# Attention loop: second halves of side work an iteration later, routing in mid-iteration, part of a weight conversion moved into the next stage

## The chip, the cores and the metric

One core of one Trainium2 chip runs the whole program. The time is device microseconds of one execution; the profile comes from one further execution with the hardware profiler on. TensorE (PE) multiplies matrices, VectorE (DVE), ScalarE (ACT) and GpSimd (POOL) work on rows, SyncE (SP) and POOL issue most of the transfers. Each engine works through its own queue in order.

## What is computed

Three layers follow one another. The first is a recurrent attention over 4 sequences of 768 tokens with 8 heads of 48:

```python
for t in range(S):
    cur = u * k_t (outer) v_t
    y_t = r_t @ (state + cur)
    state = w_t[:, None] * state + k_t (outer) v_t
```

The second is a mixture of 8 experts where each of the 3072 tokens (rows of 384) goes to the expert with the largest gate logit: `out = gate_w * (relu(x @ w1[e]) @ w2[e])`, with w1 of 384 x 1024. The third is a mixture of the same sizes in which each token goes to its two best experts by noisy logits. Inputs and outputs are float32.

## The kernel before, in words

Attention works on blocks of 128 tokens: 24 blocks (`NT`), 6 per sequence (`NC`). One loop, `for i in range(-4, NT)` in `attention`, runs as a pipeline by hand: iteration i transposes inputs of block i+3 and i+4, makes decays (two scans on VectorE) of block i+3, decayed keys and receptances ("products") of block i+2, scores of block i+1 on TensorE, their copies ("am", ScalarE) and masks (POOL), and the outputs and the state of block i: `ps` (state matmuls, line 452), `py` (line 457 from the carried state S, line 459 from the scores). `sums` writes the finished block into X, and the block's transposes (`turn`, line 497) and gate matmuls (`logits`, line 221) come one and two iterations later. The first block of a sequence has no carried state.

The order of the instructions in the text sets the order of every engine's queue there. At the end of each iteration stand the steps of `todo` and of `extra`:

- `todo` is the routing of a finished sequence b. `route1a` has four steps, in iterations 7 to 10 for the first sequence and six later for each next one: logits plus bias and the row maximum; the one-hot of the first maximum, the subtraction and the exponential (ScalarE); the ranks (small TensorE matmuls), the running count `seen` and the sum of the exponentials; the slot index. `route1c` scatters one block's rows to the table R1 (POOL).
- `extra` holds preparation of the first visit of layer two. `first_a`, `first_b`, `first_c` (from iteration `FI`) pick the largest expert of the first sequence from a count matmul (line 262). The steps in iterations `GW` are gathers of its weights w1 and w2 by POOL, that in `N0` the count of its tokens. The steps in iterations `EC` convert these weights: two squares (line 794, ScalarE), a total (two tiny TensorE matmuls, line 207), scales (VectorE) and then splits into two float16 halves, three for w1 and four for w2. A split is a ScalarE operation (line 812, the high part) and a VectorE operation (line 815, the low part). The steps in iterations `EX` fetch the visit's 448 rows: a gather by POOL (line 864), the scales (lines 195 to 199, VectorE) and four parts, each a ScalarE operation (line 226), a VectorE operation (line 227) and a transposing transfer on SP's queue (line 903).

A step with two halves returns its second half as a function. `once` calls the step and then, at once, what it returned.

After attention come seven visits of layer two (448 rows of one expert each; 8 blocks of first matmuls, line 834, then second matmuls, line 849), and then layer three. In a visit, work beside the matmuls is put into numbered slots, one after each block, and second halves run one slot later than their first. What `EC` has left of the conversion goes into the slots given to `spread`. The last sequence's routing stands in the first visit's slots 2, 3, 6 and 6.

Of the kernel before, what the change touches and what calls it, by code (L numbers as in the profile page):

```python
# [58 lines left out]
OE = 1  # L59
WI = -4  # L60
GI = (1, 2, 5, 8)
FI = 9
GW = (11, 12, 13, 16)
N0 = 15
EC = (15, 16, 17, 18, 18, 19, 20, 21, 22, 23, 23)
S1 = 3
EX = (19, 20, 20, 21, 21, 22)
FE = 1
# [15 lines left out]
def kernel(  # L84
# [163 lines left out]
    def ranks(x, m16, n, pr):  # L248

        nc.tensor.matmul(pr, tri, m16, start=True, stop=False)  # L250
        for c in range(n - 1):
            nc.tensor.matmul(pr[:, c + 1:, :], ones, bc(m16[:, c:c + 1, :], [P, n - 1 - c, E]),
                             start=False, stop=False)
        nc.tensor.matmul(pr, ones, bc(seen[x][:, None, :], [P, n, E]), start=False, stop=True)
        with nc.allow_low_precision(reason="counts up to 48 are exact"):
            sums = small.tile([P, E], F16, name="sums")
            nc.vector.tensor_reduce(sums, m16.rearrange("p c e -> p e c"), axis=AX, op=OP.add)
            nc.vector.tensor_tensor(seen[x], seen[x], sums, op=OP.add)
# [47 lines left out]
    def attention(extra):  # L306

        with ExitStack() as st:
# [173 lines left out]
            def norm(t):  # L482
                b, c = divmod(t, NC)
                sq = keep.tile([P, D], F16, name="sq")
                nc.scalar.activation(sq, row(t)[:, 0:META].bitcast(F32), AF.Square,
                                     accum_out=row(t)[:, META:ROW].bitcast(F32)[:, SS:SS + 1])
                if c == NC - 1:
                    meta = X[b % 2][:, :, META:ROW].bitcast(F32)
                    nc.gpsimd.tensor_copy(meta[:, :, 0], tok_all[:, b * NC:(b + 1) * NC])
                    nc.gpsimd.tensor_copy(meta[:, :, 2:2 + E], noise_sb[:, b * NC:(b + 1) * NC, :])  # L490
# [16 lines left out]
            def route1a(b, x):  # L507

                sh = [P, NC, E]
                if x == 0:  # L510
                    R = RB[b] = {n: small.tile(s, d, name=f"r1{n}") for n, s, d in (
                        ("lg", sh, F32), ("ex", sh, F32), ("oh16", sh, F16), ("sm", [P, NC], F32),
                        ("ri", sh, F32), ("rf", [P, NC], F32), ("idx", [P, NC], I32))}
                    nc.vector.tensor_tensor(R["lg"], pl[b % 2], bias_all[:, b * NC:(b + 1) * NC, :], op=OP.add)
                    R["mx"], R["oh"], R["fm"] = first_max(R["lg"], NC, "r1")
                    R["fm"][0]()
                    return
                R = RB[b]
                if x == 1:
                    for f in R["fm"][1:]:  # L520
                        f()
                    nc.vector.tensor_tensor(R["lg"], R["lg"], bc(R["mx"][:, :, None], sh), op=OP.subtract)
                    nc.gpsimd.tensor_copy(R["oh16"], R["oh"])
                    nc.scalar.activation(R["ex"], R["lg"], AF.Exp)
                elif x == 2:
                    ranks(0, R["oh16"], NC, pr[b % 2])
                    nc.vector.tensor_reduce(R["sm"], R["ex"], axis=AX, op=OP.add)
                    nc.vector.tensor_scalar(R["sm"], R["sm"], 1e-9, None, op0=OP.add)
                    nc.vector.reciprocal(X[b % 2][:, :, META:ROW].bitcast(F32)[:, :, 1], R["sm"])
                else:  # L530
                    nc.vector.tensor_tensor(R["ri"], pr[b % 2], bc(erow[:, None, :], sh), op=OP.add)
                    nc.vector.tensor_tensor(R["ri"], R["ri"], R["oh"], op=OP.mult)
                    nc.vector.tensor_reduce(R["rf"], R["ri"], axis=AX, op=OP.add)
                    nc.vector.tensor_copy(R["idx"], R["rf"])
# [23 lines left out]
            def at(f, t):  # L558
                if 0 <= t < NT:
                    f(t)  # L560

            for i in range(-4, NT):
                for n, g in enumerate(data):
                    if i >= GI[n]:
                        next(g, None)
                if i >= 0:
                    at(scores, i + 1)
                at(norm, i - 1)
                at(products, i + 2)
                at(decays_a, i + 3)  # L570
                if i >= 0:
                    at(scores_out, i + 1)
                    at(masks, i + 1)
                at(logits, i - LG)
                at(decays_inv, i + 3)
                at(decays_b, i + 3)
                if i == -2:
                    scores(0)
                    scores_out(0)
                    masks(0)  # L580
                    if OE:
                        keys_back(0)
                o = {-1: 0, 0: -1}.get(i, i) if OE else i
                at(outputs, o)
                at(diag, i + 2)
                at(state, o)
                at(turn, i - 1)
                if i >= KB and (i >= 0 or not OE):
                    at(keys_back, i + 1)
                at(state_out, o)  # L590
                at(diag_v, i + 2)
                at(sums, o)
                for n, t in (("kr", i + 3), ("w", i + 4)):
                    at(lambda t: transposes(t, n), t)
                if 0 <= i < KB:
                    keys_back(i + 1)
                if i == WI:
                    warm(WARM[1])
                at(loads_q, i + 3)
                if i >= -2 and i + NL + 2 <= NT:  # L600
                    load(i + NL + 2)
                if i >= 0:
                    nc.sync.dma_start(out[i * P:(i + 1) * P, :], zt)
                for at_i, f, b, x in todo:
                    if at_i == i:
                        f(b, x)
                for f in extra.get(i, []):
                    f()

            last = {"rows": [lambda: norm(NT - 1)], "turn": lambda pt: turn(NT - 1, pt),  # L610
                    "logits": [lambda t=t: logits(t) for t in range(NT - LG, NT)],
                    "route": [], "scatter": []}
# [559 lines left out]
    def layers():  # L1172
# [80 lines left out]
        steps0 = []  # L1253
# [3 lines left out]
            if callable(f):  # L1257
                f()

        def some(n):  # L1260
            for _ in range(n):
                once(steps0.pop(0))

        xsteps = []

        def begin(j, sidx):
# [2 lines left out]
        extra = {}  # L1269
# [3 lines left out]
                     (EC[0], lambda: steps0.extend(conv0()))):  # L1273
            add(extra, i, f)
        for i in EC:
            add(extra, i, lambda: some(1))
        for i in GW:
            add(extra, i, lambda: wsteps.pop(0)())
        for i in EX:
            add(extra, i, lambda: once(xsteps.pop(0)))  # L1280

        with tc.manual_schedule():
            last = attention(extra)
        with ExitStack() as st:
# [91 lines left out]
            with tc.manual_schedule():  # L1376
# [12 lines left out]
                for j in range(VISITS):  # L1389
                    hooks = {}  # L1390
                    q = max(0, j - EV + 1)
                    if j == 0:
# [11 lines left out]
                        add(hooks, S1 + 2, lambda: begin(1, early["sidx1"]))  # L1404
                        for s in XS1:
                            add(hooks, s, lambda: xsteps.pop(0)())
                        spread(hooks, steps0, (0, 1, 2, 3, 4, 5, 6))
                    else:
                        if j == 1:
                            for x, s in enumerate(T_PLAN):  # L1410
# [181 lines left out]
```

## Time and profile before

| | us |
|---|---|
| median of 3 runs | 882.61 (881.57 to 887.2) |
| the profiled execution's own time | 883.38 |
| its span, first to last instruction | 881.6 |
| TensorE busy | 841.1 (95%) |
| VectorE, ScalarE, POOL busy | 464.3, 435.0, 360.5 |
| attention's last iteration ends, first visit's first matmul | 211.06 |

The times of the rows count from the span's start. The span is 1.8 us shorter than the execution's time. The page's clock line gives TensorE's granted clock per fortieth of the span (22 us), 9 being full speed.

### The profile page before, as it was taken

The page shows a single profiled execution, that of the slowest core. Times are in us where ns is not written, and L with a number is a line of the kernel's source. Part 1 is how long each engine was busy: PE and PEld are TensorE (multiplying, and loading weights), DVE is VectorE, ACT ScalarE, POOL GpSimd, SP SyncE. Part 2 cuts the span into 40 slices and gives each one's busy share as a digit, 9 for nine tenths or more (in the row PEclk, how much of TensorE's full clock was granted, in tenths as well). Part 3 has the DMA queues.
Part 4 walks back from the last instruction along what each step waited for, and adds up shares of the span by engine and source line. Part 5 has one row for each costly group of instructions (what it writes and reads, how often), then busy time and mean ns, then how long its engine had stood idle before and what let it go on. Part 6 is the DMA issues. An engine that isn't in the chain of part 4 may idle for free.

```text
span 881.6 us, 16060 instructions
## 1 busy us (share of the span) xinstructions
PE 841.1 (95%) x6161; PEld 633.1 (72%) x6161; DVE 464.3 (53%) x1244; ACT 435.0 (49%) x819; POOL 360.5 (41%) x404
## 2 busy tenths in 40 slices
PE   7999999989999989899999999999999999999993
PEld 6989999888576566565666678667686766768672
DVE  7979779873674466458666624333332423333220
ACT  2545346554354475567776426445444634534220
POOL 7957697942333161540424642232122223212222
PEclk9999799966999989999999999999999999999997
DMA  9986487423454231743574384864756546535231
GB/s 178 196 154 148 108 223 165 157 64 89 123 184 112 57 103 42 244 127 100 194 223 94 80 249 95 229 179 101 197 102 198 90 86 176 102 54 102 56 38 20
DMA packets 195077, 115.42 MB, mean 131 GB/s; under 512 B 173499, under 2 KB 183863, under 8 KB 193585
## 3 DMA queue, kind: packets, MB, share of 16 engines
q1 hardware_dynamic: 169088, 63.82, 29.6%
q0 software_dynamic: 18224, 50.12, 22.8%
q10 hardware_dynamic: 7680, 0.38, 0.6%
q8 instruction: 50, 0.82, 0.4%
q14 instruction: 35, 0.28, 0.1%
HBM read 73.37 MB, written 30.01 MB: 117 GB/s over the span
## 4 chain that ended last, share of the span: by engine, by line
PE 86%; DVE 4%; issue 3%; ACT 2%; POOL 1%; DMA 1%; ACTq 1%; POOLq 0%; DVEq 0%
PE ph L834 33%; PE po L841 20%; PE po L849 10%; PE py L459 4%; PE pm L221 4%; PE pA L422 3%; PE py L457 2%; PE po L858 2%; PE pTk L377 1%; PE pTr L377 1%; PE pTw L377 1%; PE pA L439 1%; PE po L1112 1%; PE pA L497 1%; PE ps L452 1%
## 5 line engine op out<-in xcount | busy, mean ns | idle before, releaser
L834 PE MATMUL ph<-xT,w1h 128*128 128x320 f16 (+2 forms) x1104 | 290.9, 350 | 3.4 <-DMA xT<-xs 1.5
L959 DVE SCALAR_TENSOR_TENSOR hl<-ph,hh 128x320 f16<-128x320 f32 (+2 forms) x184 | 110.0, 599 | 238.2 <-ACT hh L958 222.0
L1150 POOL DMA_INDIRECT out_dram<-y,oidx x56 | 87.6, 1563 | 268.0 <-ACT y L1149 265.6
L834 PE MATMUL ph<-xT,w1l 128*128 128x320 f16 (+2 forms) x552 | 192.0, 348 | 1.0 <-issue 1.0
L834 PEld LDWEIGHTS <-w1h 128*128 128x128 f16 x1104 | 155.1, 146 | 45.8 <-issue 9.9
L958 ACT ACTIVATE hh<-ph 128x320 f16<-128x320 f32 (+2 forms) x184 | 95.4, 521 | 124.8 <-PE ph L834 102.2
L841 PE MATMUL po<-w2h,hh 128*128 128x384 f16 x384 | 125.2, 326 | 0.5 <-issue 0.5
L841 PE MATMUL po<-w2l,hh 128*128 128x384 f16 x384 | 125.2, 326 | 0.0
L841 PE MATMUL po<-w2h,hl 128*128 128x384 f16 x384 | 125.2, 326 | 0.0
L841 PEld LDWEIGHTS <-hh 128*128 128x128 f16 x768 | 74.2, 98 | 48.4 <-issue 1.0
L834 PEld LDWEIGHTS <-w1l 128*128 128x128 f16 x552 | 79.7, 144 | 24.6 <-issue 3.9
L1149 ACT ACTIVATE y<-po,gf 128x384 f32<-128x384 f32 (+1 forms) x56 | 31.6, 577 | 113.7 <-PE po L841 83.4
L1084 POOL DMA_INDIRECT R<-X,idx x56 | 56.3, 1006 | 22.3 <-issue 13.3
L815 DVE SCALAR_TENSOR_TENSOR w1l<-stage,ps_w,w1h 128x1024 f16<-128x1024 f32 x36 | 47.7, 1340 | 25.8 <-ACT w1h L812 25.8
L849 PE MATMUL po<-hh,w2h 128*128 128x448 f16 x168 | 59.9, 356 | 1.1 <-issue 1.1
L849 PE MATMUL po<-hl,w2h 128*128 128x448 f16 x168 | 59.8, 356 | 0.7 <-issue 0.7
L849 PE MATMUL po<-hh,w2l 128*128 128x448 f16 x168 | 59.7, 355 | 0.7 <-issue 0.7
L459 PE MATMUL py<-vt,am 128*128 128x48 f32 x384 | 59.3, 286 | 0.0
L432 POOL TENSOR_SCALAR_AFFINE_SELECT am<-am 128x512 f32<-128x512 f32 x48 | 46.6, 992 | 30.8 <-ACT am L427 30.7
L849 PEld LDWEIGHTS <-w2h 128*128 128x128 f16 x336 | 33.1, 99 | 34.6 <-issue 5.3
L459 PEld LDWEIGHTS py<-vt,am 128*128 128x128 f32 x384 | 55.8, 212 | 0.2
L841 PEld LDWEIGHTS <-hl 128*128 128x128 f16 x384 | 37.6, 98 | 24.9
(323 smaller groups left out, 1410.8 us busy)
## 6 DMA issues: line engine op xcount, KB each, us to landing
stage<-in_moe_w_dram SPq DMA_DIRECT2D x16, 1536.0 KB
ldw<-in_w_dram SPq DMA_DIRECT2D x24, 192.0 KB
ldk<-in_k_dram SPq DMA_DIRECT2D x24, 192.0 KB
ldr<-in_r_dram SPq DMA_DIRECT2D x24, 192.0 KB
vt<-in_v_dram SPq DMA_DIRECT2D x24, 192.0 KB
out_dram<-zt SPq DMA_DIRECT2D x24, 192.0 KB
R<-X,idx POOLq DMA_INDIRECT x56
xT<-xg SPq DMA_TRANSPOSE x56
```

What stands on the lines that cost most here:

```text
L221: nc.tensor.matmul(pl, xT[:, i, :], g[:, i, :], start=i == 0, stop=i == NI - 1)
L432: nc.gpsimd.affine_select(m, m, pattern=[[0, HP], [1, P]], compare_op=OP.is_gt, fill=0.0, base=0, channel_multiplier=-1)
L459: nc.tensor.matmul(PY[t][:, hp, x], AM[t][x][:, hp, :], VT[t][:, 2 * hp + x], start=c == 0, stop=c == 0 or x == 1)
L815: nc.vector.scalar_tensor_tensor(l, v, s, h, op0=OP.mult, op1=OP.subtract)
L834: nc.tensor.matmul(ph, a[:, i, :].rearrange("p (q m) -> p m q", m=NM)[:, m, :], xT[:, b, cols], start=n == 0, stop=n == 3 * NI - 1)
L841: nc.tensor.matmul(py, a[m][:, cols], b[:, m, :], start=n == 0, stop=n == 3 * NM - 1)
L849: nc.tensor.matmul(py, b[:, m, d * P:(d + 1) * P], a[m][:, cols], start=n == 0, stop=n == 3 * NM - 1)
L958: nc.scalar.activation(hh[m][:, 0:T], ph, AF.Relu)
L959: nc.vector.scalar_tensor_tensor(hl[m][:, 0:T], ph, 0.0, hh[m][:, 0:T], op0=OP.max, op1=OP.subtract)
L1084: st = nc.gpsimd.indirect_dma_start(out=R2[:, :], out_offset=bass.IndirectOffsetOnAxis(ap=R.idx[0:VP, x, h:h + 1], axis=0), in_=R.row[0:VP ...
L1149: nc.scalar.activation(y[0:n], py[0:n], AF.Copy, scale=gf[0:n, h:h + 1])
L1150: st = nc.gpsimd.indirect_dma_start(out=out[:, :], out_offset=bass.IndirectOffsetOnAxis(ap=oidx[0:n, h:h + 1], axis=0), in_=y[0:n], in_off ...
```

## The change

Second halves of the steps in `extra` are no longer run at once: the loop collects them in `second` and runs them in the middle of the next iteration, behind the scans and ahead of the outputs. The steps of `route1a` move from the iteration's end to the same place, its exponential moves from the second step to the third, and the sum and reciprocal of the exponentials from the third to the fourth. The scatters (`route1c`) stay at the end. The choice of the largest expert, its weight gathers and its count come one iteration later, and the conversion of its weights as well, with nine steps in attention instead of eleven: the total, the scales and all four splits of w2 are in the first visit, where before only the splits were, and the slots are 0, 1, 1, 2, 3, 4 instead of 0, 1, 2, 3.

```diff
-FI = 9
-GW = (11, 12, 13, 16)
-N0 = 15
-EC = (15, 16, 17, 18, 18, 19, 20, 21, 22, 23, 23)
+FI = 10
+GW = (12, 13, 14, 17)
+N0 = 16
+EC = (16, 17, 18, 19, 20, 21, 22, 23, 23)
...
                     nc.gpsimd.tensor_copy(R["oh16"], R["oh"])
+                elif x == 2:
                     nc.scalar.activation(R["ex"], R["lg"], AF.Exp)
-                elif x == 2:
                     ranks(0, R["oh16"], NC, pr[b % 2])
+                else:
                     nc.vector.tensor_reduce(R["sm"], R["ex"], axis=AX, op=OP.add)
                     nc.vector.tensor_scalar(R["sm"], R["sm"], 1e-9, None, op0=OP.add)
                     nc.vector.reciprocal(X[b % 2][:, :, META:ROW].bitcast(F32)[:, :, 1], R["sm"])
-                else:
                     nc.vector.tensor_tensor(R["ri"], pr[b % 2], bc(erow[:, None, :], sh), op=OP.add)
...
+            second = []
+
+            def flush():
+                for f in second:
+                    f()
+                second.clear()
...
                 at(decays_b, i + 3)
+                flush()
+                for at_i, f, b, x in todo:
+                    if at_i == i and f is route1a:
+                        f(b, x)
...
                 for at_i, f, b, x in todo:
-                    if at_i == i:
+                    if at_i == i and f is route1c:
                         f(b, x)
                 for f in extra.get(i, []):
-                    f()
-
+                    f = f()
+                    if callable(f):
+                        second.append(f)
+
+            flush()
...
-        def some(n):
-            for _ in range(n):
-                once(steps0.pop(0))
...
         for i in EC:
-            add(extra, i, lambda: some(1))
+            add(extra, i, lambda: steps0.pop(0)())
...
         for i in EX:
-            add(extra, i, lambda: once(xsteps.pop(0)))
+            add(extra, i, lambda: xsteps.pop(0)())
...
-                        spread(hooks, steps0, (0, 1, 2, 3, 4, 5, 6))
+                        spread(hooks, steps0, (0, 1, 1, 2, 3, 4, 5))
```

## Rows read from the trace of the kernel before

**Rows 1.** The page: busy time of each engine, and the granted clock in 40 slices.

```profile
PE 841.1 (95%) x6161; PEld 633.1 (72%) x6161; DVE 464.3 (53%) x1244; ACT 435.0 (49%) x819; POOL 360.5 (41%) x404
...
PEclk9999799966999989999999999999999999999997
```

**Rows 2.** Iterations: length; busy us of PE, PEld, DVE, ACT, POOL; PEclk; DMA share; GB/s.

```profile
127.89:135.15 7.26, 7.26 (x83) 6.89 (x82) 6.33 (x15) 3.69 (x10) 6.54 (x8) 1.00 0.94 240
...
94.33:105.88 11.55, 11.55 (x79) 11.01 (x78) 9.28 (x25) 3.28 (x9) 6.14 (x6) 0.56 0.44 103
...
143.28:150.02 6.74, 6.74 (x78) 6.40 (x78) 6.53 (x13) 3.20 (x8) 4.44 (x5) 1.00 0.57 141
156.84:164.87 8.03, 8.03 (x75) 7.66 (x74) 5.78 (x11) 4.71 (x11) 7.49 (x9) 0.79 0.71 274
164.87:174.09 9.22, 7.33 (x83) 6.89 (x82) 8.46 (x12) 3.81 (x11) 8.38 (x12) 1.00 0.13 46
174.09:184.15 10.06, 10.06 (x79) 9.53 (x78) 8.77 (x12) 4.34 (x9) 8.12 (x8) 0.66 0.25 83
184.15:195.79 11.64, 9.18 (x78) 8.62 (x77) 7.61 (x22) 7.82 (x16) 2.85 (x5) 0.75 0.11 32
195.79:204.50 8.71, 8.14 (x51) 7.65 (x50) 2.43 (x8) 3.04 (x8) 2.09 (x3) 0.50 0.34 64
204.50:211.06 6.56, 6.03 (x30) 5.95 (x31) 1.33 (x3) 2.38 (x7) 3.52 (x6) 0.50 0.54 181
211.06:214.00 2.94, 2.94 (x9) 1.39 (x9) 0.66 (x5) 0.47 (x2) 1.99 (x3) 0.53 0.18 70
```

**Rows 3.** What TensorE waited for, 80 to 260: total us, times, longest.

```profile
PE pA L497 <- ACT am L427: 2.5, 1, 2.5
PE pm L221 <- DVE r1lg L514: 1.9, 1, 1.9
...
PE pm L262 <- DVE seen L258: 1.3, 2, 0.8
```

**Rows 4.** VectorE in order of time: start, duration, instruction, idle before it.

```profile
164.91 2.85 DVE L815 SCALAR_TENSOR_TENSOR w1l<-stage,ps_w,w1h 128x1024 f16<-128x1024 f32 x1 [2.19 <-ACT w1h L812]
...
186.74 1.28 DVE L815 SCALAR_TENSOR_TENSOR w1l<-stage,ps_w,w1h 128x1024 f16<-128x1024 f32 x1 [1.35 <-ACT w1h L812]
```

**Rows 5.** ScalarE in order of time: a state copy, a split and a row part.

```profile
139.83 0.71 ACT L476 COPY S<-z 48x192 f32<-48x192 f32 x2
...
185.57 1.13 ACT L812 ACTIVATE w1h<-stage,ps_w 128x1024 f16<-128x1024 f32 x1
188.34 0.61 ACT L226 ACTIVATE xs<-xg,ps_g 112x384 f16<-112x384 f32 x1 [1.63 <-DVE ps_g L198]
```

**Rows 6.** VectorE in iterations 14 and 15: the first-maximum step, the state.

```profile
131.78 0.55 DVE L238 TENSOR_TENSOR c_r<-r1lg,mx_r 128x48 f32<-128x48 f32 x1
...
133.80 0.20 DVE L522 TENSOR_TENSOR r1lg<-r1lg,mx_r 128x48 f32<-128x48 f32 x1
...
138.61 0.36 DVE L470 TENSOR_TENSOR z<-ps,g 128x192 f32<-128x192 f32 x1
```

**Rows 7.** TensorE: first use of a state; first matmul of the second visit.

```profile
143.77 0.46 PE L457 MATMUL py<-S,RT 128*128 128x96 f32 x2
...
243.18 0.54 PE L834 MATMUL ph<-xT,w1h 128*128 128x448 f16 x2 [1.46 <-DMA xT<-xs]
```

**Rows 8.** POOL issues the row gathers of the first and second visit.

```profile
176.21 1.85 POOL L864 DMA_INDIRECT xg<-R,ev_sidx  x1
...
226.41 1.00 POOL L864 DMA_INDIRECT xg<-R,ev_sidx  x1 [3.78 <-DVE ev_n L1226]
```

**Rows 9.** A stretch of 2 us behind the first visit's gather, as rows 2.

```profile
180.00:182.00 2.00, 2.00 (x12) 1.67 (x12) 1.97 (x4) 0.56 (x1) 0.38 (x2) 0.50 0.73 299
```

**Rows 10.** VectorE in the first visit: scales and last row half for the second.

```profile
231.76 0.17 DVE L195 TENSOR_SCALAR pe_g<-xg 128x4 int32<-128x4 int32 x1 [1.58 <-DMA xg<-R,ev_sidx]
...
240.09 0.62 DVE L227 SCALAR_TENSOR_TENSOR xs<-xg,ps_g,xs 112x384 f16<-112x384 f32 x1
```

## The prediction

> **What bounds the kernel now.** I read the page's busy line and its clock line first [rows 1]. TensorE is busy for 95% of the span, so a change pays only where TensorE stands still or runs at its lower clock, and the clock line is low most often in the first quarter, which holds the attention loop. There I cut the trace at the first state matmul of each iteration and asked for busy time and granted clock of each piece [rows 2]. An undisturbed iteration takes 7.26 us (iteration 14) at clock 1.00, and 6.74 (iteration 16) where the four transposes of the keys are left out, so four transposes are 0.52. Against that the reader is to see three things: iteration 10 with 11.55 us at clock 0.56; iterations 12 and 18, the first of a sequence, which are alike and stand with one row, 8.03 at 0.79 with TensorE busy throughout; and iterations 19 to 23, which take 46.2 us together, with the clock at 0.50 over the last two. Then I listed what TensorE waited for [rows 3]: no wait over 2.5 us, but low clock follows them. Last I followed the queues of VectorE and ScalarE in iterations 18 to 21 [rows 4, 5].
>
> **Why they are late there.** Each step that splits w1 has a ScalarE half and a VectorE half that follows at once. VectorE stands 2.19 us for ScalarE, then takes 2.85 us, and all that is behind it is late [rows 4]; there are three such waits, of which the first and the last are shown. In iteration 19 the routing's subtract-and-max is behind that, and TensorE's next gate matmul waits 1.9 us for it [rows 3]. At the end of iteration 20 it is a ping-pong: VectorE waits 1.35 us for the split, only then makes the scales of the first visit's rows, ScalarE waits 1.63 us for these [rows 5], and the copies of the scores ("am") behind that hold TensorE's transposes for 2.5 us [rows 3]. After that the clock is half until the first visit.
>
> **The change, part by part**, against the profiled execution (883.38 us; the median of the runs is 0.8 lower).
>
> *First expert an iteration later.* The count matmul stood right behind the ranks, at the ends of iterations 9 and 15, and waited for VectorE's "seen": 1.3 us in two waits, 0.8 and 0.5 [rows 3]. Routing now comes half an iteration earlier and the count a full one later, so both waits go: 1.3 us. Behind the first the clock fell: iteration 10 has the work of iteration 16, so 11.55 - 6.74 = 4.8 us go if the fall was the wait's. The four weight gathers move an iteration later on POOL's queue. POOL is nearly full in iterations 18 and 19 (7.49 of 8.03, 8.38 of 9.22 [rows 2]), so it drags a backlog, but by then the same transfers have been issued in both kernels: nothing.
>
> *VectorE's halves an iteration later.* VectorE's three waits go, and the halves run in iterations 21 to 23, which have fewer products and scans. Iteration 19 falls from 9.22 to 7.26 (2.0). Iteration 20 has one group of transposes less: 10.06 to 6.74 (3.3). Iteration 21 has three groups less and the ranks (about 0.3): 7.26 - 1.56 + 0.3, about 6.0 instead of 11.64. On the old time axis iteration 20 then begins at 172.1, 21 at 178.9, 22 at 184.9.
>
> *What is late next.* VectorE now comes to the row scales much earlier, right behind the sums of iteration 20. In iteration 14 the routing starts, behind the sums, 3.9 us after the iteration's start; with 2.2 us of routing put ahead of them [rows 6] that is 172.1 + 6.1 = 178.2. But the rows are not there: POOL issues their gather at 176.21 [rows 8], and data still come at 299 GB/s in the stretch to 182 [rows 9], a landing 5.8 us after the issue; for the second visit it is 226.41 to 231.76, 5.4 us [rows 8, 10]. The issue took 1.85 there against 1.00 in the visit, so POOL may come 0.9 earlier; the rows land between 180.6 and 182, and VectorE stands 2.4 to 3.8 us. Behind it are some 5 us of its usual work and the split's half before the state of iteration 21 is out, near 186.7 with ScalarE's copy, where TensorE's output matmuls want it at 185.4: about 1 us. ScalarE waits for the scales too, and the copies of the scores behind it hold the transposes of iteration 21 by another 0.7 to 1.2. A third wait of about 1 us comes at iteration 23, where the state copy is behind two row halves (0.62 each [rows 10]), a split's half (1.28 [rows 4]) and routing.
>
> *The end of attention.* The last ScalarE half, VectorE half, row half, transpose and landing form a chain; from the end of the last row half to the first matmul it is 240.71 to 243.18 in the second visit, 2.5 us [rows 7, 10]. Without a fall of the clock the state copy of iteration 23 is out at 192.9, and two ScalarE halves (1.13 and 0.61), two VectorE halves (1.28 and 0.62) and these 2.5, partly overlapping, put the first matmul of the first visit at 198.4 instead of 211.06: 12.7 us less. With a fall at the end of iteration 21 the last two iterations take their present 15.3 us [rows 2], some 4 us of scores and gate matmuls stand ahead of them from 184 on, and it comes at 203.3: 7.8 less. I take a fall within iteration 22, at 202.1: 9.0, nearer to the second because the new waits stand where [rows 2] shows falls. The first visit begins at half clock now (2.94 us at 0.53 [rows 2]); after a wait for rows it will do so for a little longer, up to twice that: 0.8 taken off. On SP's queue the four row transposes pass a few zero writes and nothing else waits there: nothing.
>
> *Routing mid-iteration.* It puts 2.2 us (131.78 to 134.0) ahead of the state update. In the next iteration that update ends at 138.97 [rows 6], ScalarE's copy takes 0.71 [rows 5], and the state is used at 143.77 [rows 7]: 4.1 us of cover, of which 1.9 are left. Cost nothing; with the cover gone it is rival three. The exponential moves to the next step, so ScalarE no longer waits for it; in the first visit it stands in one slot with its sum, at most half a us of VectorE.
>
> *w2 in the first visit.* Its sum (two tiny matmuls), three small VectorE operations and the first split come a slot later, and the others with it. TensorE waits for nothing in that visit until 241.7 [rows 7], and the second half of the matmuls begins three slots behind the last split. Between 0 and 0.5; I take 0.
>
> **Sum:** 1.3 + 4.8 + 9.0 - 0.8 = 14.3; of 883.38 that leaves 869.1, on the median's basis 868.3. **Forecast 868.5.**
>
> **The rivals.** *One: the clock falls whatever the waits.* For it: iterations 12 and 18 fall with no idle at all, and the last iterations have few transposes to keep the array dense. Against it: iteration 15 has the same ranks with a shorter wait, and iteration 16 behind it stays at 1.00 [rows 2]. Then 1.3 us remain, and what iterations 19 and 20 give before a fall at the start of iteration 21 (first matmul at 206.4, 4.7 less): 6.0, so 876.6. The Trainium skill ("TensorE: Matmul & The Clock Gate", Part 1, the HAM clock gate) holds that the clock is gated down after TensorE has been idle for a spell, which a gap of 0.8 us hardly is; by that rule the fall in iteration 10 was not the wait's and would come back, as in this rival. The trace does not settle it: it shows a fall behind 0.8 us and falls behind none. Chance 0.20.
>
> *Two: the gathered rows become the bound.* If they land after 182, VectorE's stand is over 3.8 us, the scores' copies and the state of iteration 21 hold TensorE for 2 us or more, and the clock falls inside iteration 21. The first matmul comes near 206: 5 less instead of 9.0. With 1.3 + 4.8 that makes 11.1: 871.5. For it speaks POOL's backlog, against it the shorter issue. Chance 0.14.
>
> *Three, slower: routing ahead of the state.* If POOL stretches scans and routing beyond the cover, TensorE waits before its output matmuls in each iteration with the first-maximum step (8, 14, 20), and a fall like that of iteration 10 follows: 0.8 + 4.8 each, 17 us. The end stays at half clock as now, and only the 6.1 of the first part is saved: 893.5. It decides from 1.9 us of stretch, nearly the routing's own length again. Chance 0.06.
>
> That the halves are not deferred at all I give nothing: the three splits and four row parts return their second half, and only these.
>
> **How the numbers follow.** Forecast 0.60, rivals 0.20, 0.14, 0.06. The forecast's own range is 863.8 (no fall before iteration 23) to 872. Adding rival two and most of rival one: 862 to 878.5. Within 1% of 882.6 (about what a measurement of this kernel tells from no change) begins at 873.8: faster is 0.95 of the forecast, most of rival two and little of rival one, 0.67; same 0.27; slower 0.06.
>
> **What would show it.** Right: no wait for "seen"; iteration 10 at 6.7 to 7.3 us and clock 1.00; no VectorE wait for the split w1; VectorE's scale operation waiting for the gather; the first matmul of the first visit 12 to 19 us earlier than now. Wrong: iteration 10 at half clock again; TensorE idle before output matmuls in iterations 8, 14 or 20; iterations 21 to 23 again over 25 us together; or the first visit longer than its 30.5 us up to the wait for the second visit's rows.

## The result, and the profile after

The changed kernel takes 876.88 us (median of 11 runs, 870.34 to 879.4), the kernel before 883.17 beside it (11 runs, 880.48 to 887.2): ratio 0.9894 [0.9865, 0.9922], faster by 1.1%. The profiled execution took 870.34, the fastest of the 11; its span is 868.5 us at a mean granted clock of 0.970, against 883.38, 881.6 and 0.954 before. So what the profile shows is the changed kernel at its best: 13.0 us less, where the medians give 6.3 and the ratio 9.4 (0.0106 x 883.17). Here and below a ratio is taken over the fast runs alone, those within 1.5% of the kernel's fastest, while a median holds every run; on the third chip of the experiments this leaves 11 of 29 runs of the kernel before out of the ratios.

The page after, to be read beside [rows 1]: TensorE's busy time is 12.8 us less, and the clock line, which before falls to 7, 6 and 6 in slices 5, 9 and 10, stays at 8 or above in the first quarter (8 in slices 6, 9 and 10).

```profile
PE 828.3 (95%) x6161; PEld 621.0 (72%) x6161; DVE 472.1 (54%) x1244; ACT 436.1 (50%) x819; POOL 362.3 (42%) x404
...
PEclk9999989988999989999999999999999999999997
```

The span times the granted clock is 841.0 before and 842.4 after. At full clock the two profiled executions would be equally long; their difference is time at half clock (881.6 x 0.046 = 40.6 and 868.5 x 0.030 = 26.1).

Iterations of the changed kernel in the columns of [rows 2]: 10, 13, 18 to 23, and the start of the first visit.

```profile
92.40:99.66 7.26, 6.96 (x80) 6.61 (x80) 6.92 (x19) 3.13 (x9) 5.38 (x6) 1.00 0.64 138
...
113.58:124.33 10.75, 10.57 (x81) 9.97 (x82) 9.36 (x15) 6.30 (x16) 10.12 (x10) 0.68 0.65 160
...
153.36:159.79 6.43, 6.43 (x76) 6.16 (x75) 6.29 (x11) 2.81 (x9) 5.59 (x6) 1.00 0.42 156
159.79:168.67 8.88, 7.74 (x83) 7.04 (x82) 8.21 (x17) 5.16 (x12) 8.30 (x11) 1.00 0.56 202
168.67:179.19 10.52, 10.44 (x85) 9.77 (x84) 9.17 (x14) 4.18 (x10) 10.20 (x14) 0.68 0.30 99
179.19:185.88 6.69, 6.50 (x73) 5.87 (x70) 6.03 (x13) 4.21 (x11) 3.75 (x4) 1.00 0.11 26
185.88:192.52 6.64, 4.62 (x51) 4.25 (x50) 4.85 (x13) 4.87 (x12) 2.45 (x3) 0.90 0.33 85
192.52:199.11 6.59, 6.02 (x27) 5.76 (x28) 2.76 (x4) 2.66 (x6) 4.09 (x5) 0.50 0.62 210
199.11:202.05 2.94, 2.94 (x10) 1.51 (x10) 0.06 (x2) 2.94 (x5) 1.99 (x3) 0.59 0.18 70
```

Iteration 10 runs at full clock, iterations 21 and 22 take 13.3 us instead of 20.4, and the first visit starts at 199.11 instead of 211.06. Half clock is still there, in iterations 13, 20 and 23.

What TensorE waited for, 80 to 260, in the columns of [rows 3]:

```profile
PE py L457 <- ACT S L476: 1.6, 3, 1.3
...
PE pm L221 <- DVE pe_w L195: 0.8, 1, 0.8
PE pm L221 <- DVE r1ri L531: 0.8, 1, 0.8
PE ps L452 <- DVE z L470: 0.8, 1, 0.8
...
PE pm L221 <- DVE cnt_half L264: 0.6, 1, 0.6
PE pm L221 <- DVE cnt_first L264: 0.3, 1, 0.3
```

The waits of [rows 3] for am (2.5), r1lg (1.9) and seen (1.3) are gone; shorter ones stand in their place, two kinds for the state (S, z) and four of gate matmuls (line 221). `pe_w`, `r1ri` and the counts are what VectorE makes from other columns of the PSUM tile `pm` that the gate matmul writes, so in this program it waits for reads of results that it does not touch.

VectorE in order of time, as [rows 4, 10] (the low part of a split is line 829 here, the scales of the gathered rows line 195), and POOL's gather, as [rows 8]:

```profile
104.51 1.97 DVE L239 SCALAR_TENSOR_TENSOR c_ev<-c_ev,eio 128x8 f32<-128x8 f32 x1
...
169.21 3.46 DVE L386 TENSOR_TENSOR_SCAN g<-w,d1r 128x516 f32<-128x516 f32 x1
...
179.44 0.54 DVE L195 TENSOR_SCALAR pe_g<-xg 128x4 int32<-128x4 int32 x1 [1.40 <-DMA xg<-R,ev_sidx]
...
181.37 1.27 DVE L829 SCALAR_TENSOR_TENSOR w1l<-stage,ps_w,w1h 128x1024 f16<-128x1024 f32 x1
...
187.13 1.28 DVE L829 SCALAR_TENSOR_TENSOR w1l<-stage,ps_w,w1h 128x1024 f16<-128x1024 f32 x1 [1.49 <-ACT w1h L826]
...
193.67 1.28 DVE L829 SCALAR_TENSOR_TENSOR w1l<-stage,ps_w,w1h 128x1024 f16<-128x1024 f32 x1 [1.49 <-issue]
```

```profile
173.62 1.75 POOL L878 DMA_INDIRECT xg<-R,ev_sidx  x1 [0.16 <-issue]
```

The splits no longer hold up anything in iteration 21. VectorE now stands 1.40 us for the gathered rows, which land 5.8 us after the issue began, and the split of iteration 22 still waits 1.49 for its high part.

### The profile page after: what moved, and what is told of

It is laid out like the page before. It is cut to its first block, busy times and chain, and to the rows that moved or that the text cites. A ratio compares the mean times of both kernels' runs of the same rounds, so it can differ in the third digit from the quotient of the medians.

```text
span 868.5 us, 16068 instructions
## 1 busy us (share of the span) xinstructions
PE 828.3 (95%) x6161; PEld 621.0 (72%) x6161; DVE 472.1 (54%) x1244; ACT 436.1 (50%) x819; POOL 362.3 (42%) x404
## 4 chain that ended last, share of the span: by engine, by line
PE 76%; DVE 9%; POOL 4%; issue 4%; ACT 3%; DMA 2%; another core or an unknown queue 1%; ACTq 0%; POOLq 0%; SPq 0%; DVEq 0%
PE ph L848 33%; PE po L855 21%; PE po L863 10%; PE pm L221 2%; PE po L872 2%; DVE g L386 2%; PE py L459 2%; DVE e L396 1%; PE py L457 1%; PE pA L422 1%; PE po L1126 1%; POOL R L537 1%; POOL am L432 1%; POOL av L414 1%
## 5 line engine op out<-in xcount | busy, mean ns | idle before, releaser
L829 DVE SCALAR_TENSOR_TENSOR w1l<-stage,ps_w,w1h 128x1024 f16<-128x1024 f32 x36 | 45.5, 1281 | 23.5 <-ACT w1h L826 22.0
L459 PE MATMUL py<-vt,am 128*128 128x48 f32 x384 | 57.2, 278 | 0.2 <-POOL am L432 0.2
L459 PEld LDWEIGHTS py<-vt,am 128*128 128x128 f32 x384 | 53.1, 203 | 0.8 <-POOL am L432 0.5
L432 POOL TENSOR_SCALAR_AFFINE_SELECT am<-am 128x512 f32<-128x512 f32 x48 | 41.3, 884 | 17.5 <-ACT am L427 17.4
```

What stands on the lines that cost most here:

```text
L432: nc.gpsimd.affine_select(m, m, pattern=[[0, HP], [1, P]], compare_op=OP.is_gt, fill=0.0, base=0, channel_multiplier=-1)
L459: nc.tensor.matmul(PY[t][:, hp, x], AM[t][x][:, hp, :], VT[t][:, 2 * hp + x], start=c == 0, stop=c == 0 or x == 1)
L829: nc.vector.scalar_tensor_tensor(l, v, s, h, op0=OP.mult, op1=OP.subtract)
```

## The experiments

The theory behind the forecast: TensorE's waits make the clock fall, so fewer waits give less time at half clock. Its rival: the clock falls in these stretches whatever the waits. The runs were made on three chips that differ by up to 3% for the kernel before, so each kernel is set against runs of the kernel before on its own chip only. In the table a run's span times (1 - granted clock) is called its low-clock cost, the remainder its time at full clock; both are means over the runs that the ratio compares, and estimates, since they take all work to follow TensorE's clock.

| kernel | ratio to before, 95% | median | full clock | low-clock cost |
|---|---|---|---|---|
| first chip: before | | 891.91 | 846.0 | 42.7 |
| first expert later alone | 0.9988 [0.9955, 1.0021] | 889.43 | 845.7 | 41.5 |
| second halves later alone | 0.9934 [0.9901, 0.9967] | 882.55 | 844.2 | 37.8 |
| routing mid-iteration alone | 0.9962 [0.9931, 0.9993] | 887.07 | 843.5 | 41.3 |
| w2 in the first visit alone | 1.0006 [0.9975, 1.0037] | 892.16 | 846.0 | 43.2 |
| second chip: before | | 885.07 | 843.0 | 40.2 |
| the change again | 0.9911 [0.9882, 0.9940] | 876.28 | 839.1 | 34.3 |
| state first | 0.9851 [0.9815, 0.9887] | 869.65 | 842.2 | 26.5 |
| reads in mid-iteration | 0.9903 [0.9870, 0.9937] | 876.67 | 838.7 | 36.1 |
| both | 0.9874 [0.9838, 0.9909] | 872.95 | 841.2 | 29.2 |
| third chip: before | | 868.86 | 831.5 | 31.6 |
| state first, dense | 0.9938 [0.9897, 0.9979] | 858.46 | 832.8 | 24.0 |
| state first again | 0.9943 [0.9898, 0.9987] | 861.02 | 830.4 | 27.4 |
| reads in mid-iteration again | 0.9936 [0.9889, 0.9984] | 861.15 | 830.5 | 26.8 |
| both again | 0.9896 [0.9827, 0.9964] | 854.09 | 829.1 | 24.4 |

No line is read from the profiles of "reads in mid-iteration", "both" and "both again", whose spans are 969.2, 4042.7 and 866.9 us.

**One part at a time.** First the later first expert:

```diff
-FI = 9
-GW = (11, 12, 13, 16)
-N0 = 15
+FI = 10
+GW = (12, 13, 14, 17)
+N0 = 16
```

> The kernel before with one part alone: the first expert, its weight gathers and its count an iteration later. Theory A (the waits cost, and the clock falls behind them): no TensorE wait for seen (1.3 us) and iteration 10 at full clock (4.8 us): ratio about 0.993, 6 us less. Theory B (the clock falls whatever the waits): 1.3 us less, ratio 0.9985, and iteration 10 or a neighbour at half clock. Under both the end of attention stays as before: iterations 19 to 23 take about 46 us. What may spoil A: the small VectorE steps that pick the expert now stand at the end of iteration 11, ahead of iteration 12, where the changed kernel showed a wait of 0.8 us for the state and a fall.

No difference can be measured. The wait for `seen` goes, and the count matmul, now an iteration later, waits longer than before for VectorE's slot index, which reads `pm`; the clock falls behind that, from the end of iteration 10 through 11 (waits of 80 to 260, and a stretch in the columns of [rows 2]):

```profile
PE pm L262 <- DVE r1ri L531: 3.1, 2, 1.6
...
99.00:110.00 11.00, 10.45 (x60) 10.26 (x57) 9.02 (x23) 2.94 (x7) 8.61 (x11) 0.54 0.46 110
```

So the 6.1 us that the forecast gave this part are not in the part alone. What it is worth beside the earlier routing, where this wait of 3.1 us does not occur, was not tried. The expectation failed in another place: iterations 19 to 23, which this kernel leaves as they were, take 38.8 us in its profile (166.22 to 205.01), not 46.

Second, the halves alone:

```diff
                 at(decays_b, i + 3)
+                flush()
...
                 for f in extra.get(i, []):
-                    f()
+                    f = f()
+                    if callable(f):
+                        second.append(f)
...
```

> The kernel before with one part alone: VectorE's halves of the side steps an iteration later, in the middle. Theory A: the three VectorE waits for the w1 split (5.3 us) go, TensorE's waits of 1.9 and 2.5 us shrink to under 1 each, and iterations 19 to 23 take about 38 to 40 us instead of 46: ratio about 0.992, 6 to 8 us less; iteration 10 stays at half clock. Theory B: only the idle time goes, 3 to 4 us, and the last iterations are at half clock as before: ratio 0.996.

This is the largest part. Its iterations 19, 20, 21, and 22 with 23, in the columns of [rows 2], with the waits for `seen`:

```profile
168.74:176.00 7.26, 7.26 (x82) 6.90 (x81) 7.12 (x13) 4.81 (x12) 6.95 (x9) 1.00 0.16 59
176.00:182.82 6.82, 6.82 (x79) 6.46 (x78) 6.61 (x12) 3.09 (x9) 6.57 (x7) 1.00 0.38 123
182.82:189.80 6.98, 6.89 (x77) 6.21 (x76) 6.04 (x18) 6.17 (x12) 2.78 (x5) 1.00 0.19 54
189.80:201.05 11.25, 10.14 (x80) 9.85 (x79) 4.36 (x12) 6.96 (x18) 5.51 (x8) 0.74 0.52 152
...
PE pm L262 <- DVE seen L258: 3.8, 2, 2.2
```

Iterations 19 to 23 take 32.3 us instead of 46.2, and the lengths 7.26 and 6.82 are those that the forecast worked out (7.26 and 6.74). Iteration 10 stays at half clock, behind the waits for `seen`, as expected. But 46.2 is one profile: in those of the first and the fourth part alone the same iterations, unchanged, take 38.8 us, and against these the gain is 6.5. The median gains 9.4 us (891.91 - 882.55) and the ratio 5.9 (0.0066 x 891.91); its interval holds the figures of both theories, 0.992 and 0.996.

Third, routing alone:

```diff
...
                 at(decays_b, i + 3)
+                for at_i, f, b, x in todo:
+                    if at_i == i and f is route1a:
+                        f(b, x)
...
                 for at_i, f, b, x in todo:
-                    if at_i == i:
+                    if at_i == i and f is route1c:
```

The move of the exponential and of its sum by a step is in it too.

> The kernel before with one part alone: routing in mid-iteration, the exponential and its sum a step later. Theory A: the ranks come half an iteration before the count, so the waits for seen go here too (1.3 us) and iteration 10 keeps its clock: about 6 us less, ratio 0.993; the last iterations change little, since the w1 halves still block VectorE. Theory B: 1 to 2 us less, ratio 0.998. If routing ahead of the state costs (rival three of the prediction), TensorE idles before the output matmuls of iterations 8 and 14 and the time rises by 5 us or more.

A small gain, between the two theories, in full-clock time (2.5 us) and hardly in low-clock cost. In its profile the waits for `seen` are gone and iteration 10 keeps its clock, as theory A had it, but the clock falls elsewhere. Routing ahead of the state does bring waits for the state and for what follows it, as rival three had it, though not in iterations 8 and 14:

```profile
PE py L459 <- POOL am L432: 1.8, 2, 1.6
PE py L457 <- ACT S L476: 1.6, 2, 1.4
PE pm L250 <- POOL r1oh L523: 1.6, 1, 1.6
...
PE ps L452 <- DVE z L470: 1.2, 2, 0.6
```

The longest of the first three stand at 111.88, 145.29 and 177.66, and the clock is at half soon after each (from 114.5, 148.5 and 179.5).

Fourth, w2 alone:

```diff
-EC = (15, 16, 17, 18, 18, 19, 20, 21, 22, 23, 23)
+EC = (15, 16, 17, 18, 18, 19, 20, 21, 22)
...
-                        spread(hooks, steps0, (0, 1, 2, 3, 4, 5, 6))
+                        spread(hooks, steps0, (0, 1, 1, 2, 3, 4, 5))
```

> The kernel before with one part alone: the total, the scales and the first split of w2 in the first visit. Both theories: nothing, ratio 0.999 to 1.001; TensorE waits nowhere in the first visit until the second visit's rows, and the tiny matmuls leave the end of attention (0.2 us).

Nothing, as forecast. The kernel is worth more for something else: up to iteration 22 its attention is that of the kernel before. TensorE's count matmul in iteration 9 of the kernel before, which came right ahead of the fall in iteration 10 [rows 2]:

```profile
92.38 0.17 PE L262 MATMUL pm<-seen,ones 128*128 128x8 f16 x1 [0.77 <-DVE seen L258]
```

The same instruction and the iteration after it, but for its last half us, in this kernel:

```profile
91.83 0.17 PE L262 MATMUL pm<-seen,ones 128*128 128x8 f16 x1 [1.56 <-DVE seen L258]
...
93.95:100.20 6.25, 6.25 (x74) 5.91 (x73) 6.08 (x12) 2.15 (x6) 3.08 (x5) 1.00 0.55 125
```

The wait is twice as long, and the clock does not fall. Its attention ends at 207.90, 3.2 us earlier than in the profile of before. One profile's falls, even behind a wait, are not properties of the schedule. Nor is the length of a wait: the two that the prediction put at the head of the end of attention, 1.9 and 2.5 us [rows 3], are here

```profile
PE pm L221 <- DVE r1lg L514: 0.8, 1, 0.8
...
PE pA L497 <- ACT am L427: 0.5, 1, 0.5
```

with the same instructions up to there, and iterations 19 to 23 take 38.8 us (169.09 to 207.90). The four parts' ratios add up to 1.1% (0.12 + 0.66 + 0.38 - 0.06), what the whole change gives; but each is known to 0.3% only, so that no part needs another is not shown.

**The change again, and its new waits taken away.** The changed kernel as it is:

> The changed kernel itself once more, to stand beside the next three on the same chip and to see how far one kernel's runs differ. Span times (1 - mean clock) is what the low clock cost a run; span times clock is what would be left at full clock. Theory A: against the kernel before on this chip about 2 us less at full clock and 7 to 9 us less low-clock cost, ratio 0.988 to 0.991. Theory B: the low-clock cost is the same as before within 2 us. Both: within one kernel the runs differ by the low clock alone, at a full-clock time steady to 2 us, and the profile shows falls at other places than the first profile of this kernel.

The ratio repeats, with 5.9 us less low-clock cost and 3.9 us less at full clock. Against the expectation the full-clock time is not steady to 2 us: it goes from 835.3 to 842.0 in the 7 runs. As expected, the falls are at other places: the clock is at half from about 107 to 111, 131 to 138, 168 to 175 and 185 to 203, where the first profile of the same kernel has 116 to 123, 170 to 178 and 191 to 201. In this profile too the gate matmul waits 0.8 us for `pe_w` at the end of iteration 19, and the clock falls at 168.6; the other waits differ (TensorE's, 80 to 260):

```profile
PE pm L250 <- POOL r1oh L523: 1.5, 1, 1.5
PE pm L221 <- DVE pe_w L195: 0.8, 1, 0.8
```

State first: the second halves and the routing behind the state update instead of ahead of it.

```diff
                 at(decays_b, i + 3)
-                flush()
-                for at_i, f, b, x in todo:
-                    if at_i == i and f is route1a:
-                        f(b, x)
...
+                flush()
+                for at_i, f, b, x in todo:
+                    if at_i == i and f is route1a:
+                        f(b, x)
```

> The changed kernel with the deferred halves and the routing put behind the state update in the middle of the iteration instead of ahead of it. Theory A (as in the prediction's third new wait): the wait of 1.3 us for the state at iteration 23 and of 0.2 to 0.8 at iteration 13 shrink; 1 to 3 us less than the changed kernel. Rival: the state has cover, and what waits then is the sums, the score copies or the row transposes, which come later by the same amount: no difference, or 1 to 2 us more at the end of attention.

On this chip its low-clock cost is 7.8 us under that of the changed kernel and its full-clock time 3.1 over, and the intervals of the two overlap by 0.0005. The waits for the state are gone, as theory A had it, but its waits are not fewer, only others:

```profile
PE pm L221 <- DVE cnt_half L264: 1.7, 1, 1.7
...
PE pm L221 <- DVE r1ri L531: 1.4, 1, 1.4
PE py L457 <- DVE X L479: 1.4, 2, 1.0
PE pm L221 <- DVE cnt_first L264: 0.8, 1, 0.8
```

Reads in mid-iteration: VectorE's reads of `pm` for the first expert and the scales are handed back as second halves, so that no gate matmul stands right behind them.

```diff
-FI = 10
+FI = 9
...
-        for i, f in ((FI, first_a), (FI + 1, first_b), (FI + 1, first_c), (GW[0], weights0), (N0, first_d),
+        for i, f in ((FI, lambda: first_a), (FI + 1, first_b), (FI + 2, first_c), (GW[0], weights0), (N0, lambda: first_d),
...
-        for i in EC:
-            add(extra, i, lambda: steps0.pop(0)())
+        for n, i in enumerate(EC):
+            add(extra, i, (lambda: steps0.pop(0)) if n == 3 else (lambda: steps0.pop(0)()))
```

> The changed kernel with every step whose VectorE half reads a small result from the shared PSUM tile pm (the two counts, the scales of w1) run whole in mid-iteration, one after the gate matmuls instead of right ahead of them, and the choice of the expert spread over iterations 10 to 11. Theory A: TensorE's gate matmuls no longer wait for cnt_first, cnt_half and pe_w (1.7 us), nor the state matmuls of iteration 13 (0.8), and the falls behind them go in part: 2 us less at full clock, 2 to 5 us less low-clock cost, ratio to the changed kernel about 0.994. Theory B: 2 us less, the low-clock cost unchanged.

Not told apart from the change (0.9903 and 0.9911), and its low-clock cost is no lower (36.1 and 34.3). That taking these waits away gives less half clock is not borne out; the profile of its repeat, below, shows that others came in their place, so it does not test what fewer waits would give.

Both edits in one kernel:

> Both edits of the two runs before together. Theory A: their sum, 3 to 7 us less than the changed kernel, about 0.982 to 0.986 of the kernel before. Theory B: 3 us less than the changed kernel.

Between the two, and told apart from neither.

**Repeated on the third chip**, with one kernel more: state first with eight matmuls of 128 x 128 ones beside the gate matmuls of seven iterations, where TensorE's work is thin. Nothing uses their result.

```diff
+DENSE = (6, 12, 18, 20, 21, 22, 23)
...
+                if i in DENSE:
+                    for _ in range(8):
+                        nc.tensor.matmul(pm[:, 384:512], ones, ones, start=True, stop=True)
```

> The kernel of e6_state_first with eight extra 128x128 float16 matmuls on constants behind the gate matmuls of iterations 6, 12, 18 and 20 to 23 (their result is read by nobody). They cost 56 x 0.055, about 3.1 us at full clock. If falls follow thin work on TensorE, the falls in these iterations become fewer and the low-clock cost drops by more than 5 us: ratio to e6_state_first 0.997 or less. If they follow waits alone, the low-clock cost is the same and the time 3 us more, ratio 1.003.

> The kernel of e6_state_first once more, beside the others on this chip: if its gain over the changed kernel is real, its ratio to the kernel before is again 0.983 to 0.988 with a low-clock cost some 10 us or more under that of the kernel before; if it was chance, 0.990 to 0.992.

Both kernels have falls at the same two places, about 147 and 194 (and one each elsewhere, at 130 with the extra matmuls and at 102 without). First the dense kernel's two stretches, then state first's, in the columns of [rows 2]:

```profile
147.00:158.00 11.00, 10.72 (x53) 10.39 (x55) 8.45 (x21) 2.93 (x7) 8.54 (x9) 0.53 0.67 191
195.00:206.00 11.00, 10.43 (x48) 8.09 (x46) 2.69 (x5) 5.18 (x12) 6.03 (x8) 0.53 0.53 176
```

```profile
146.00:157.00 11.00, 9.28 (x52) 9.09 (x49) 8.66 (x22) 3.15 (x8) 8.46 (x10) 0.53 0.68 186
194.00:202.00 8.00, 7.43 (x35) 5.85 (x35) 1.98 (x5) 3.59 (x7) 5.28 (x8) 0.57 0.58 199
```

The fall at 147 begins between iterations 16 and 17, which have no extra matmuls, so only that at 194 tests them: the eight of iteration 22 come at 188.24, and the clock falls all the same, behind a wait of 1.4 us. The whole loop, up to the first visit, in the two profiles:

```profile
0.00:201.29 201.29, 188.58 (x1945) 177.03 (x1946) 172.49 (x307) 96.36 (x217) 156.18 (x197) 0.93 0.69 160
```

```profile
0.00:199.02 199.02, 182.15 (x1889) 171.29 (x1890) 173.34 (x307) 96.67 (x217) 153.58 (x197) 0.95 0.69 162
```

Here the extra matmuls do not keep the clock up. Over all runs the low-clock cost is 3.4 us lower with them and the full-clock time 2.4 higher; that lies between the two forecasts (over 5 lower, or no lower), and the ratios are not told apart. So the part of thin work stays open. The gain of state first, 0.9851 on the second chip, is 0.9943 here (0.9910 by the medians), and the two intervals do not meet: its lead over the change is not confirmed. Its low-clock cost is 4.2 us under that of the kernel before, not 10. (The change itself was not run on this chip.)

> The kernel of e7_reads_mid once more, for its profile. If falls follow waits of 0.5 us and more, a profile with hardly any such wait in iterations 7 to 20 has no falls there, and the low-clock cost is well under that of the changed kernel. If not, falls stand in it with no wait ahead of them, in iterations 9 to 21, and the ratio is again near 0.990.

The condition does not hold. The waits for the counts and `pe_w` are gone, but others are there, 5.5 us in all from 80 to 260 without those of the visits, where the changed kernel's two profiles have 5.1 and 2.9:

```profile
PE pm L250 <- POOL r1oh L523: 1.9, 1, 1.9
...
PE py L457 <- ACT S L476: 1.4, 2, 1.3
PE pm L221 <- DVE r1ri L531: 0.8, 1, 0.8
```

Two of its three falls (130 and 191) come right behind these, and one (157.5) behind no wait, as the second branch has it. The low-clock cost, 26.8 us, was not compared with that of the change on this chip.

> The kernel of e8_both once more: state first, and the small reads in mid-iteration. Theory A: fewer waits than e10_state_first_again by 2 to 3 us and a lower cost of the clock, ratio to it 0.995. Theory B: the same time as it within 2 us.

Between its two theories the runs do not decide: its ratio is 0.9953 of that of state first again (0.9896 and 0.9943), but the two intervals overlap. All four stand at 0.990 to 0.994; "both" (0.9874, 0.9896) and "reads in mid-iteration" (0.9903, 0.9936) repeat within their intervals on the other chip, and state first does not. "Both" may be a little better than the change; the runs do not show it, as its intervals overlap the change's 0.9894 and 0.9911.

In the changed kernel's first two profiles the 0.8 us for `pe_w` stood ahead of a fall in iteration 20 (170.6 and 168.6). In the profiles of state first (twice), dense and reads in mid-iteration again that wait is gone, and none falls there. So a wait can go with a fall; but the clock then falls elsewhere (130, 147, 157, 195). Over the eleven profiles that are read, the kernel before's first among them, 39 falls begin between 57 us and the first visit: 34 of them in or within 5 us behind a wait of TensorE of 0.4 us or more, 5 behind none. Yet 20 waits of that size, the longest 1.56 us, have no fall behind them. (0.4 and 5 us are bounds of this count, no more.) So falls mostly come behind waits, and which wait is followed by one no row here tells.

## Why the prediction was right, and where it was not

The sign and the range were right: 876.88 lies in 862 to 878.5. The forecast of 868.5 was 8.4 us too low, and the time lies outside the forecast's own range (863.8 to 872); what holds it is the part of the range that was added for the rivals. Whether it is faster by more than 1% is not settled: the ratio says 1.06%, its interval 0.8 to 1.35%, and the medians 0.7%, on the "same" side of the prediction's 873.8.

*First expert and iteration 10* (1.3 + 4.8). Iteration 10 came down to 7.26 at clock 1.00, and the waits for `seen` went, as written. But the step "4.8 us go if the fall was the wait's" failed: with the wait twice as long there is no fall in the w2 kernel, with the count moved there is one anyway, and in the changed kernel it came back in iteration 13 (10.75 at 0.68). Up to the start of iteration 18 the profile gains 3.5 us (156.84 against 153.36), not 6.1, and the part alone is worth 1.1 us with an interval from -1.9 to 4.0 (0.0012 x 891.91). The Trainium skill ("TensorE: Matmul & The Clock Gate", Part 1, the HAM clock gate), which I set against this term, has the clock gated down after a spell of idleness. That a wait of 1.56 us led to no fall agrees; that the clock fell in iteration 10 behind 0.77 us shows that short idleness does not rule a fall out either. The same section of the Trainium skill says that the monitor's look at TensorE is not in step with the kernel, so that runs of one kernel differ. The runs here do differ, from 870.34 to 879.4 us at clocks of 0.970 to 0.958; that this is why, none of them shows.

*The end of attention* (9.0). From iteration 18's start to the first visit 54.2 us became 45.8: 8.5 us. That is near 9.0 by luck: 1.6 of it is iteration 18, which I took as falling always (8.03 at 0.79) and which ran at 6.43 and full clock, and from iteration 19 on, which is what the 9.0 stood for, it is 6.9 (46.2 and 39.3). Iteration 19 took 8.88 instead of 7.26. Iteration 20, for which I had 6.74, took 10.52 behind the 0.8 us for `pe_w`; I had named what the scales of the rows wait for, and not that the scales of w1, now an iteration later and alone at an iteration's end, are read out of the gate matmuls' tile. That the deferral does what the arithmetic says is shown by the kernel with it alone: iterations 19 and 20 at 7.26 and 6.82. One sign of being right did not come: VectorE still waits once for the split (1.49 us at 187.13).

*New waits.* VectorE's stand for the gathered rows came, 1.4 us instead of 2.4 to 3.8. Times must be counted from the start of iteration 20 here, as the profile is 3.5 us ahead of the old time axis by iteration 18: VectorE was there 9.4 us after it (178.04 - 168.67), not 6.1, as the iteration ran mostly at half clock; POOL issued the gather 4.95 us after it, not 3.2 to 4.1; and the rows landed after 10.8, not 8.5 to 9.9. Both were late, VectorE more so. The 1 us for the state of iteration 23 came as 1.3. The one at iteration 22 (1 us) and that of iteration 21's transposes (0.7 to 1.2) did not come.

*First visit.* The 0.8 us that I took off for a longer half clock are not there: the clock of its first 2.94 us is 0.59, against 0.53 before [rows 2].

*Routing and w2.* Zero for w2 is what it gave. Routing has 0.38% [0.07, 0.69], which I had at nothing; its cost was seen as well, in waits for the state of up to 1.4 us in the kernel with it alone.

*The rivals.* Rival two did not decide (1.4 us, not over 3.8), and rival three's iterations 8, 14 and 20 show no wait for the state in the changed kernel. Rival one gave 876.6, and the median is 876.88. That it came out for rival one's reason is not shown: the profile, of the fastest run, has the first visit 12 us earlier, which was not in it, and no run near a median was profiled. But that falls come at changing places is nearer to what the experiments show than a fall that belongs to iteration 10.

**The failing step** is the sum's use of half-clock stretches, which made the forecast 14.3 us where the ratio gives 9.4 and the medians 6.3. Most of the 14.3 are falls read from one execution and taken as belonging to their place: 4.8 in iteration 10, and of the end of attention the half-clock shares of iterations 20 and 21 (10.06 x 0.34 and 11.64 x 0.25 [rows 2], 6.3). In the profiles the attention loops gain 12.0, in the runs the whole kernel 9.4 [6.9, 11.9]. In the 11 runs of the changed kernel the span rises by 0.85 us with each us of low-clock cost (correlation 0.92): a run's place between 870 and 879 is mostly how much half clock it had. What the change lowers is the mean of that, and the time at full clock too, which the first pair of profiles does not show: on the second chip by 5.9 and 3.9 us. What sets the half clock is open. Most falls stand behind a wait, but the sum of the waits does not set it: the profiles of state first have more of them (5.6 and 7.8 us from 80 to 260, without the visits') than those of the changed kernel (5.1 and 2.9), and on the second chip its low-clock cost is lower (26.5 and 34.3). Whether thin work has a part, the dense kernel does not settle.

## What to carry to other kernels

Where the clock falls and recovers within a loop, price a change from the iterations at full clock, and count falls as an average over executions, not at the place where one profile shows them. A second profile of the same schedule tells what is the schedule's: iterations 19 to 23 of the old order took 46.2 us in one and 38.8 in two others. A long second half behind its first on one queue is worth deferring by an iteration. Before a read of a shared PSUM tile is moved, look at which matmul writes that tile next: the wait moves with the read.

## What was not expected of the hardware

VectorE's scans got slower with the new order: the same 24 scans of each kind took 8.0 us more in all. Before:

```profile
L396 DVE TENSOR_TENSOR_SCAN e<-w,d1f 128x516 f32<-128x516 f32 x24 | 33.4, 1391 | 0.8
L386 DVE TENSOR_TENSOR_SCAN g<-w,d1r 128x516 f32<-128x516 f32 x24 | 32.0, 1331 | 4.9 <-ACT w L379 4.9
```

After:

```profile
L386 DVE TENSOR_TENSOR_SCAN g<-w,d1r 128x516 f32<-128x516 f32 x24 | 36.8, 1535 | 5.6 <-ACT w L379 5.6
L396 DVE TENSOR_TENSOR_SCAN e<-w,d1f 128x516 f32<-128x516 f32 x24 | 36.6, 1526 | 0.8
```

That is the whole rise of VectorE's busy time (464.3 to 472.1). It repeats: the same sums are 72.5 us in the second profile of the changed kernel, 69.0 with routing alone, 67.5 with the halves alone, and 65.9 and 66.1 with the other two parts alone. The longest, 3.46 us at 169.21 against 1.22 for the shortest, lies beside POOL operations without a break; that POOL is the cause was not tried apart, and other scans beside POOL took 1.22. An 8-column operation took 1.97 us (104.51); from there VectorE does not stand still until it has made the state of iteration 12 (113.17), the 0.8 us wait ahead of iteration 13's fall.
